# Transposes moved ahead of the scale columns, and a norm ahead of their read, in the first phase of a fused attention and MLP kernel

## Chip, cores, metric

One core of one Trainium2 chip. The time is device time in microseconds (us) of one execution. "Granted clock" is the share of its full clock that the profile says TensorE was given; "landing" is the time at which the last completion record of a transfer came in. TensorE (PE) does matmuls and transposes, VectorE (DVE), ScalarE (ACT) and GpSimd (POOL) do elementwise work, SyncE (SP) issues transfers.

## The reference

A transformer block with modulation (2048 rows of 1024, 32 query heads, 4 key/value heads, bf16):

```python
mod = (_silu(c) @ w_mod).reshape(c.shape[0], 6, 1, -1)
sa, ca, ga, sb, cb, gb = (mod[:, i] for i in range(6))      # shortened
h = _layernorm(x) * (1 + ca) + sa
x = x + ga * A(h)            # q = h @ wq, windowed attention, @ wo
h = _layernorm(x) * (1 + cb) + sb
x = x + gb * B(h)            # silu(h @ w_gate) * (h @ w_up) @ w_down
```

What matters is the start: the layernorm of the first 512 rows (four row tiles of 128), its transpose, the scale columns 1 + ca, and the first q projection.

## The kernel before

The first transfers go to one queue in this order. The first load holds row tiles 0 and 1, the second tiles 2 and 3, and `load_wm(1, 0)` is a megabyte of w_mod for the first half of ca:

```python
for i in range(QT // 2):
    load_x2(i)
for half in range(DH):
    load_wm(1, half)
    load_wq8(2 * half)
    load_wq8(2 * half + 1)
load_wm(0, 0)
...
load_wm(0, 1)
```

The stretch that is changed. `norm_*(t, half)` norms half of tile t, `xpose_0(t, n, half)` is four PE transposes (L962), `mod_cols` is 32 one-column matmuls (L786) and a VectorE read of their result (L789), `warm` issues dummy matmuls, `h_scale` (L1045) makes the operand of q:

```python
norm_pool(1, m1[:, 4:5], slice(0, 512))
...
norm_dve(2, 0)
warm(2)
rstd_0(mv[3])
norm_act(1, m1[:, 5:6], 1)
xn_tile(3)
norm_dve(3, 0)
mod_cols(1, 0, ca1, True)          # waits for the first megabyte of w_mod
...
norm_dve(2, 1)
norm_act(3, m3[:, 4:5], 1)
xpose_0(1, xn0[1], 0)
xpose_0(2, xn0[2], 0)
xpose_0(3, xn0[3], 0)
xpose_0(1, xn0[1], 1)
...
h_scale(0, h0_ps[0][:, 0, :])      # needs the columns and all first-half transposes
...
for dt in range(4):
    for g in range(4, H0):
        q0(g, (dt,))               # the q projection, L1065
```

The instructions keep this order on each engine.

Of the kernel before, what the change touches and what calls it, by code (L numbers as in the profile page):

```python
# [588 lines left out]
def fast_path(ctx, tc, flag, A_x, A_k_cache, A_v_cache, A_wq, A_wo, B_x, B_w_gate, B_w_up,  # L589
# [59 lines left out]
    def mm(name, shape=(P, 512), dt=FP32):  # L649
        return psp.tile(list(shape), dt, name=name, tag="mm", bufs=4)  # L650
# [107 lines left out]
    def warm(n):  # L758
        for _ in range(n):
            nc.tensor.matmul(warm_ps, lhsT=ones_bf, rhs=warm_w, start=True, stop=True)  # L760
# [20 lines left out]
    def mod_cols(vec, half, dst, add_one, tiles=(0, 1, 2, 3)):  # L781
        wm = wm_tiles[(vec, half)]
        ps = mm("mod_ps", (P, 4))
        for i in tiles:
            for dt in range(DT):
                nc.tensor.matmul(ps[:, i:i + 1], lhsT=wm[:, dt, i * P:(i + 1) * P],  # L786
                                 rhs=siluc[:, dt:dt + 1], start=(dt == 0), stop=(dt == DT - 1))
        i0, i1 = tiles[0], tiles[-1] + 1
        nc.vector.tensor_scalar(out=dst[:, 4 * half + i0:4 * half + i1], in0=ps[:, i0:i1],  # L789
                                scalar1=1.0 if add_one else 0.0, scalar2=None, op0=ALU.add)  # L790
# [168 lines left out]
    def xpose_0(t, n, half):  # L959
        for i in range(4):  # L960
            dt = 4 * half + i
            nc.tensor.transpose(h0_ps[half][:, i, t * P:(t + 1) * P],  # L962
                                n[:, dt * P:(dt + 1) * P], ident)
# [5 lines left out]
    xn0 = {}  # L969

    def rstd_0(m):
        nc.scalar.activation(out=m[..., 2:3], in_=m[..., 1:2], func=ACT.Ln, bias=eps_t)
        nc.scalar.activation(out=m[..., 2:3], in_=m[..., 2:3], func=ACT.Exp, scale=-0.5)

    def xn_tile(t):
        xn0[t] = wk.tile([P, D], BF16, name="xn", tag="xn", bufs=3)

    def norm_dve(t, half):
        sl = slice(half * 512, half * 512 + 512)
        nc.vector.tensor_scalar(out=xn0[t][:, sl], in0=xt[t][:, sl], scalar1=mv[t][:, 0:1],  # L980
                                scalar2=mv[t][:, 2:3], op0=ALU.subtract, op1=ALU.mult)
# [5 lines left out]
    def norm_act(t, minus, half):  # L987
        sl = slice(half * 512, half * 512 + 512)
        nc.scalar.activation(out=xn0[t][:, sl], in_=xt[t][:, sl], func=ACT.Identity, bias=minus,
                             scale=mv[t][:, 2:3])  # L990
# [23 lines left out]
    for t in (1, 2):  # L1014
# [3 lines left out]
                            op0=ALU.mult, op1=ALU.mult)  # L1018
    norm_dve(2, 0)
    warm(2)  # L1020
    rstd_0(mv[3])
    norm_act(1, m1[:, 5:6], 1)
    xn_tile(3)
    norm_dve(3, 0)
    mod_cols(1, 0, ca1, True)
    nc.gpsimd.tensor_scalar(out=m3[:, 4:5], in0=mv[3][:, 0:1], scalar1=-1.0, scalar2=mv[3][:, 2:3],
                            op0=ALU.mult, op1=ALU.mult)
    norm_dve(2, 1)
    norm_act(3, m3[:, 4:5], 1)
    xpose_0(1, xn0[1], 0)  # L1030
    xpose_0(2, xn0[2], 0)
    xpose_0(3, xn0[3], 0)
    xpose_0(1, xn0[1], 1)
    xpose_0(2, xn0[2], 1)
# [432 lines left out]
def kernel(tc, *args):  # L1467
    nc = tc.nc
    with tc.tile_pool(name="guard", bufs=1) as gp:
        flag = gp.tile([1, 1], I32, name="flag")  # L1470
        over = fast_path(tc, flag, *args)
        with tc.If(over > 0):
            general_path(tc, *args)
# [30 lines left out]
```

## Time and profile before

| | before |
|---|---|
| median of the first three runs | 1271.33 us (1271.32 to 1271.65) |
| the run whose profile is shown | 1271.83 us, span 1270.0 us |
| PE busy, granted clock | 1262.1 us, 0.999 |
| all PE waits | 3.3 us, all before 9.7 us |

### The profile page before, as it was taken

The page shows a single profiled execution, that of the slowest core. Times are in us where ns is not written, and L with a number is a line of the kernel's source. Part 1 is how long each engine was busy: PE and PEld are TensorE (multiplying, and loading weights), DVE is VectorE, ACT ScalarE, POOL GpSimd, SP SyncE. Part 2 cuts the span into 40 slices and gives each one's busy share as a digit, 9 for nine tenths or more (in the row PEclk, how much of TensorE's full clock was granted, in tenths as well). Part 3 has the DMA queues.
Part 4 walks back from the last instruction along what each step waited for, and adds up shares of the span by engine and source line. Part 5 has one row for each costly group of instructions (what it writes and reads, how often), then busy time and mean ns, then how long its engine had stood idle before and what let it go on. Part 6 is the DMA issues. An engine that isn't in the chain of part 4 may idle for free.

```text
span 1270.0 us, 18153 instructions
## 1 busy us (share of the span) xinstructions
PE 1262.1 (99%) x7587; PEld 641.2 (50%) x7587; DVE 609.0 (48%) x1331; ACT 336.3 (26%) x440; POOL 4.3 (0%) x17
## 2 busy tenths in 40 slices
PE   8999999999999999999999999999999999999998
PEld 4555555555555555555554444444444444444444
DVE  5665658785678664677564631311222112221122
ACT  4543334343333433334341111011100111011100
POOL 1000000000000000000000000000000000000000
PEclk9999999999999999999999999999999999999999
DMA  9897657678556655455585479336633565425702
GB/s 292 206 259 171 168 141 176 168 162 211 128 136 175 150 137 153 113 154 113 120 206 143 137 225 248 95 95 208 215 114 105 169 213 182 158 91 169 246 16 70
DMA packets 306763, 204.45 MB, mean 161 GB/s; under 512 B 145521, under 2 KB 303217, under 8 KB 306674
## 3 DMA queue, kind: packets, MB, share of 16 engines
q1 hardware_dynamic: 301762, 199.03, 58.2%
q10 hardware_dynamic: 4912, 4.20, 1.0%
q8 instruction: 61, 1.00, 0.3%
q14 instruction: 28, 0.23, 0.1%
HBM read 165.94 MB, written 4.21 MB: 134 GB/s over the span
## 4 chain that ended last, share of the span: by engine, by line
PE 99%; DMA 1%; SPq 0%; DVE 0%; issue 0%
PE gu_ps L1380 30%; PE a_ps L1298 17%; PE q_ps L1223 16%; PE d_ps L1400 15%; PE o_ps L1266 9%; PE s_ps L1234 9%; PE q_ps L1065 1%; DMA wm<-in_w_mod_dram 1%; PE mod_ps L786 0%; PE one_ps L1083 0%; PE h_ps L962 0%; PE one_ps L1076 0%; SPq L664 0%; PE q_ps L1129 0%; DVE f L1404 0%
## 5 line engine op out<-in xcount | busy, mean ns | idle before, releaser
L1236 ACT ACTIVATE pT<-s_ps 128x1024 bf16<-128x1024 f32 x256 | 249.4, 1020 | 347.5 <-PE s_ps L1234 347.5
L1298 PE MATMUL a_ps<-wo,oT 128*128 128x512 bf16 x1024 | 241.9, 379 | 0.0
L1223 PE MATMUL q_ps<-hT,wq 128*128 128x512 bf16 x960 | 227.1, 379 | 0.0
L1386 DVE TENSOR_TENSOR guT<-gu_ps,sg 128x512 bf16<-128x512 f32 x112 | 77.5, 692 | 287.8 <-ACT sg L1385 287.8
L1380 PE MATMUL gu_ps<-hT,wg 128*128 128x512 bf16 x896 | 211.7, 379 | 0.0
L1385 ACT ACTIVATE sg<-gu_ps 128x512 bf16<-128x512 f32 x112 | 66.9, 597 | 488.7 <-PE gu_ps L1380 482.9
L1400 PE MATMUL d_ps<-wd,guT 128*128 128x512 bf16 (+2 forms) x952 | 194.2, 366 | 0.0
L1380 PE MATMUL gu_ps<-hT,wu 128*128 128x512 bf16 x672 | 163.3, 379 | 0.0
L1298 PEld LDWEIGHTS <-oT 128*128 128x128 bf16 x1024 | 100.2, 98 | 120.6
L947 DVE CAST qT<-q_ps 128x512 bf16<-128x512 f32 x121 | 83.6, 691 | 154.7 <-PE q_ps L1223 154.4
L1223 PEld LDWEIGHTS <-wq 128*128 128x128 bf16 x960 | 93.9, 98 | 113.3
L1400 PEld LDWEIGHTS <-guT 128*128 128x128 bf16 x952 | 90.9, 98 | 102.9
L1266 PEld LDWEIGHTS <-pT 128*128 128x128 bf16 x2048 | 126.6, 98 | 30.2
L1380 PEld LDWEIGHTS <-wg 128*128 128x128 bf16 x896 | 87.7, 98 | 105.5
L1266 PE MATMUL o_ps<-v_sb,pT 128*128 128x129 bf16 x2048 | 137.0, 220 | 0.0
L1234 PE MATMUL s_ps<-qT,kT 128*128 128x512 bf16 x512 | 131.5, 379 | 0.0
L1380 PEld LDWEIGHTS <-wu 128*128 128x128 bf16 x672 | 65.7, 98 | 79.3
L1253 DVE TENSOR_TENSOR oq<-o_ps,rl 128x256 bf16<-128x256 f32 (+2 forms) x256 | 100.6, 419 | 3.9
L1404 DVE TENSOR_TENSOR f<-d_ps,gb_bc 128x512 f32<-128x512 f32 (+2 forms) x34 | 22.4, 660 | 140.8 <-PE d_ps L1400 140.8
L1234 PEld LDWEIGHTS <-kT 128*128 128x128 bf16 x512 | 44.9, 98 | 30.9 <-issue 0.5
L1306 DVE TENSOR_TENSOR acc<-a_ps,acc 128x512 f32<-128x512 f32 x64 | 44.0, 688 | 32.6 <-PE a_ps L1298 32.6
L1380 PE MATMUL gu_ps<-hT,v_sb 128*128 128x512 bf16 x224 | 57.5, 379 | 0.0
(106 smaller groups left out, 427.0 us busy)
## 6 DMA issues: line engine op xcount, KB each, us to landing
wq<-in_A_wq_dram SPq DMA_DIRECT2D x64, 512.0 KB
wo<-in_A_wo_dram SPq DMA_DIRECT2D x64, 512.0 KB
wg<-in_B_w_gate_dram SPq DMA_DIRECT2D x56, 512.0 KB
wd<-in_B_w_down_dram SPq DMA_DIRECT2D x56, 512.0 KB
wu<-in_B_w_up_dram SPq DMA_DIRECT2D x42, 512.0 KB
v_sb<-in_B_w_up_dram SPq DMA_DIRECT2D x14, 512.0 KB
x<-in_A_x_dram SPq DMA_DIRECT2D x8, 512.0 KB
wm<-in_w_mod_dram SPq DMA_DIRECT2D x4, 1024.0 KB
```

What stands on the lines that cost most here:

```text
L947: nc.vector.tensor_copy(out=t, in_=q_ps)
L1223: nc.tensor.matmul(q_ps, lhsT=w, rhs=hT[("h1", cc)][:, dt, :], start=(dt == 0), stop=(dt == DT - 1))
L1234: nc.tensor.matmul(s_ps[:, i, :], lhsT=kT[:, kv, j * P:(j + 1) * P], rhs=qT[g], start=True, stop=True)
L1236: nc.scalar.activation(out=p[:, 2 * jj:2 * jj + 2, :], in_=s_ps, func=ACT.Exp, scale=scale)
L1253: nc.vector.tensor_tensor(out=dst, in0=ps[:, s0:s0 + cnt, 0:Dh], in1=sc, op=ALU.mult)
L1266: nc.tensor.matmul(o_slot["ps"][:, s_, :], lhsT=pT[g][:, j, t * P:(t + 1) * P], rhs=v_sb[:, kv, j, 0:VN], start=(j == 0), stop=(j == WT - 1))
L1298: nc.tensor.matmul(a_ps, lhsT=oT[(cc, 2 * q + i)][:, hh % 4, t * P:(t + 1) * P], rhs=wo_tiles[(cc, q, dh, i)][:, hh % 4, :], start=(hh == ...
L1306: nc.vector.tensor_tensor(out=acc[(cc, t)][:, dsl], in0=a_ps, in1=acc[(cc, t)][:, dsl], op=ALU.add)
L1380: nc.tensor.matmul(ps[:, n, :], lhsT=gu_w[(cc, fg, nm, dt // 4)][:, dt % 4, fi * P:(fi + 1) * P], rhs=hT[("h2", cc)][:, dt, :], start=(dt ...
L1385: nc.scalar.activation(out=g, in_=ps[:, 0, :], func=ACT.Silu)
L1386: nc.vector.tensor_tensor(out=guT[(cc, fg)][:, fi, :], in0=ps[:, 1, :], in1=g, op=ALU.mult)
L1400: nc.tensor.matmul(d_ps, lhsT=guT[(cc, f // 4)][:, f % 4, t * P:(t + 1) * P], rhs=wd_tiles[(cc, dh, f // 4)][:, f % 4, c0:c0 + w], start=( ...
```

## The change

The intent is to do ready transposes while PE waits for the w_mod block, and to keep VectorE from holding up the scaling.

```diff
     norm_dve(2, 0)
     warm(2)
+    xpose_0(1, xn0[1], 0)
+    xpose_0(2, xn0[2], 0)
     rstd_0(mv[3])
     norm_act(1, m1[:, 5:6], 1)
     xn_tile(3)
     norm_dve(3, 0)
+    norm_dve(2, 1)
     mod_cols(1, 0, ca1, True)
     nc.gpsimd.tensor_scalar(out=m3[:, 4:5], ...)   # cut
-    norm_dve(2, 1)
     norm_act(3, m3[:, 4:5], 1)
-    xpose_0(1, xn0[1], 0)
-    xpose_0(2, xn0[2], 0)
     xpose_0(3, xn0[3], 0)
```

## The prediction

> **What bounds the kernel now.** I read the busy shares first, then who waited for whom, then the chain that ended last, then the timeline of the stretch that the diff touches. The page's first part says which engine sets the end:
>
> ```profile
> PE 1262.1 (99%) x7587; PEld 641.2 (50%) x7587; DVE 609.0 (48%) x1331; ACT 336.3 (26%) x440; POOL 4.3 (0%) x17
> ```
>
> TensorE (PE) is busy for 1262.1 of 1270.0 us. About 3.3 us of the rest are three waits, which are all that the list of waits, filtered to PE, has for the whole span (columns: engine, line and tile, releaser, us in total, times, longest):
>
> ```profile
> PE warm_ps L760 <- DVE warm_w L749: 1.6, 1, 1.6
> PE h_ps L962 <- POOL xn L984: 1.1, 1, 1.1
> PE mod_ps L786 <- DMA wm<-in_w_mod_dram: 0.6, 1, 0.6
> ```
>
> All three lie in the first 10 us. After 9.68 us PE waits for nothing until its last matmul. So an instruction there can be worth something in one way only: PE must reach the point from which it runs unbroken sooner, and nothing later may take that back. The chain that ended last, in its stretch from 9 us on (start, duration, what), shows how this point is reached:
>
> ```profile
> 1.74 7.90 DMA wm<-in_w_mod_dram
> 9.64 0.04 issue
> 9.68 0.95 PE mod_ps L786 x32
> 10.63 1.36 PE h_ps L962 x24
> 12.00 4.38 PE q_ps L1065 x20
> ```
>
> The first megabyte of w_mod lands at 9.64 us. Then follow the 32 tiny matmuls that make half of the scale columns (L786), then 24 transposes of the normed rows (L962), then the q projection (L1065). This is the stretch in question. Its timeline (start, duration, engine, line, operation, output<-input, shapes, count, idle before):
>
> ```profile
> 8.38 0.77 POOL L984 TENSOR_SCALAR xn<-x,mv 128x512 bf16<-128x512 bf16 x1 [0.43 <-ACT mv L973]
> ...
> 8.72 0.58 DVE L980 TENSOR_SCALAR xn<-x,mv 128x512 bf16<-128x512 bf16 x1
> ...
> 9.46 0.42 DVE L980 TENSOR_SCALAR xn<-x,mv 128x512 bf16<-128x512 bf16 x1 [0.16 <-POOL mv L1017]
> 9.46 1.52 ACT L989 ACTIVATE xn<-x,mv 128x512 bf16<-128x512 bf16 x2
> ...
> 9.68 0.95 PE L786 MATMUL mod_ps<-siluc,wm 128*128 128x1 bf16 x32 [0.62 <-DMA wm<-in_w_mod_dram]
> ...
> 10.50 1.50 PE L962 MATMUL h_ps<-ident,xn 128*128 128x128 bf16 x24
> 10.67 0.16 DVE L789 TENSOR_SCALAR modT<-mod_ps 128x4 f32<-128x4 f32 x1 [0.80 <-PE mod_ps L786]
> 10.75 0.40 DVE L980 TENSOR_SCALAR xn<-x,mv 128x512 bf16<-128x512 bf16 x1
> 11.37 1.27 DVE L1045 TENSOR_SCALAR hs<-h_ps,modT 128x512 bf16<-128x512 bf16 x3 [0.21 <-PE h_ps L962]
> ...
> 11.90 0.59 PE L1065 MATMUL q_ps<-hs,wq 128*128 128x512 bf16 x2
> ```
>
> The first-half norm of row tile 1 (POOL) is done at 8.38 + 0.77 = 9.15 us and that of tile 2 (VectorE) at 8.72 + 0.58 = 9.30 us. Their transposes could run from there, but stand in PE's order behind the L786 group, which waits for its weights until 9.68 us. PE is idle for 0.62 us beside ready work.
>
> **What the Trainium skill says.** "TensorE: Matmul & The Clock Gate", Part 2, "Step-by-step: what each phase is for", has weight loads pulled ahead of running matmuls, but the matmuls themselves in program order. The trace agrees: the ready transposes stayed behind the waiting L786. The same page, Part 1, "Wait — 56ns, not 53.3ns?", gives about 56 ns from start to start of warm 128-column matmuls and a floor of about 25 ns for very small ones. The trace agrees roughly: (11.90 - 10.50) / 24 = 58 ns for the transposes, (10.50 - 9.68) / 32 = 26 ns for L786. Part 4, "PE-mode transpose", has about 275 ns for a transpose within a kernel and says that the fast clock does not engage for it; here the 32 transposes have a median of 219 ns at a granted clock of 1.00, so I take the trace. The same page, "Engine queue depths", calls VectorE strictly first in, first out; that agrees with the tile 2 norm at 10.75 us, right behind the read of L789, though VectorE had nothing to do from 9.88 to 10.67 us.
>
> **The change part by part.** No instruction is added or removed. The listing of instruction order shows eight transposes (with their eight weight loads) moved ahead of the L786 group on PE, one norm moved ahead of the L789 read on VectorE, and ACT, POOL and the DMA queue in the same order.
>
> 1. Eight transposes go into the gap. POOL released PE earlier in the trace within 0.05 us (7.95 to 8.00), so they start at about 9.15 + 0.05 = 9.20 us. At 57 ns each, the last starts at 9.20 + 7 x 0.057 = 9.60 us, and PE is free for the next at about 9.66 us. The first of tile 2 is due at 9.43 us, after its data (9.30). L786 thus starts at 9.68 us as before, when its weights are there: the eight are hidden. Cost 0 to 0.03 us.
> 2. After L786, 16 transposes remain instead of 24: PE could begin q at 10.50 + 16 x 0.058 = 11.43 us instead of 11.90 us, 0.47 us sooner.
> 3. VectorE must follow, since q reads what L1045 writes. Before, L1045 began at 11.37 us, when the twelfth transpose was done (10.50 + 11 x 0.057 + 0.22 = 11.35). Now only the four first-half transposes of tile 3 follow L786: 10.50 + 3 x 0.057 + 0.22 = 10.89 us. The other condition is the read of the columns, 10.67 + 0.16 = 10.83 us; where the same read is followed by its user with nothing between (17.19 + 0.16 = 17.35, user at 17.46), 0.11 us pass, so 10.94 us. This one ends last. L1045 starts at 10.94 instead of 11.37 us: 0.43 us sooner.
> 4. That needs VectorE free, hence the moved norm. It takes 0.40 us at 9.88 to 10.28 us, in idle time, instead of 10.75 to 11.15 us. Left where it was, it would hold L1045 until about 11.15 us and half the gain would be lost.
> 5. One L1045 takes 0.48 us and PE started 0.05 us after its end (11.37 + 0.48 = 11.85, q at 11.90). New start of q: 10.94 + 0.48 + 0.05 = 11.47 us. The smaller of 0.47 and 0.43 counts: PE starts its unbroken run 0.43 us sooner. Sum: 1271.33 - 0.43 = 1270.90 us.
>
> **The rivals.**
> (a) A later transfer takes the place of the wait. The w_mod and wq loads go on at 340 to 385 GB/s and don't come sooner because PE is sooner. The trace's completion records (I read these times directly; no printed view lists them) have the next blocks landing at 10.99 and 12.38 (wq), 15.38 (w_mod), 21.68 and 24.78 us (w_mod), and PE's first weight loads from them at 11.78, 12.98, 16.00, 22.41 and 25.40 us: slack 0.79, 0.60, 0.62, 0.74 and 0.62 us. All exceed 0.43, by 0.17 us at the least. For it: a transfer that lands 0.3 us later in some run would give back 0.1 us. Against it: PE has no such wait now. If true, 1271.0 to 1271.2 us.
> (b) The eight transposes start late and push L786 past 9.68 us. POOL's spans are rough. If PE saw tile 1 only at 9.40 us, L786 would move by 0.2 us, the column read with it, and 0.2 us would be left: 1271.1 us. If the POOL wait were longer than the DMA wait, it would be the new first wait and the time could rise; with 9.15 against 9.68 us I see no sign of it.
> (c) The start is bought but given back later, where VectorE, ACT or the DMA queue pace PE. PE is 99% busy and has no wait after 9.68 us, which speaks against it. Loads that reuse a buffer are issued when PE releases it, so they move along; those that don't are the ones in (a). If true, 1271.3 us, no change.
> (d) The gain is larger, as a full 0.62 us of idle time is filled. Against it: only eight transposes, 8 x 0.057 = 0.46 us, are put there. At most 1270.85 us.
>
> **Range and chances.** The point is step 5. The three runs before span 0.33 us (1271.32 to 1271.65) and the median sits at the low end, so the reading itself can be off by 0.15 us either way. Rivals (a) and (b) move it up by 0.1 to 0.3 us; (d) down by 0.05 us. I take 1270.60 to 1271.35 us, which holds a complete loss of the gain at its upper end. 2% is 25 us; nothing in this change is in reach of it in either direction, and I leave half a per cent on each side for what I have not seen.
>
> **What would show it right or wrong.** In the profile after: eight L962 at about 9.20 us, their wait named POOL; L786 still at 9.68 to 9.71 us, idle before it under 0.1 us in place of 0.62; three L980 on VectorE before L789; L1045 at 10.94 us; the first q matmul at 11.47 us; every later piece of the chain 0.43 us sooner, and no new PE wait. Step 1 is wrong if L786 starts after 9.75 us; step 3 if L1045 starts near 11.1 us or later; rival (a) is right if PE waits for wm or wq after 12 us; rival (c) if q starts at 11.5 us but the last matmul does not end 0.4 us sooner.

## The result, and the profile after

| six runs each, same rounds | median | lowest to highest |
|---|---|---|
| before | 1271.42 us | 1271.27 to 1273.02 |
| after | 1271.66 us | 1271.43 to 1272.19 |

The ratio is 1.000 with a 95% interval of 0.9987 to 1.0013. Ratios and intervals are worked out from the runs of the same rounds; they are not the ratio of the medians. The prediction of 1270.90 us was wrong: 1271.66 lies above its range, and no gain is to be seen.

Yet the profile after looks as predicted. Its timeline over the same stretch:

```profile
8.31 0.77 POOL L984 TENSOR_SCALAR xn<-x,mv 128x512 bf16<-128x512 bf16 x1 [0.43 <-ACT mv L973]
...
9.14 0.62 PE L962 MATMUL h_ps<-ident,xn 128*128 128x128 bf16 x8 [0.15 <-POOL xn L984]
9.39 0.74 DVE L980 TENSOR_SCALAR xn<-x,mv 128x512 bf16<-128x512 bf16 x2 [0.16 <-POOL mv L1017]
...
9.60 0.94 PE L786 MATMUL mod_ps<-siluc,wm 128*128 128x1 bf16 x32
...
10.40 1.05 PE L962 MATMUL h_ps<-ident,xn 128*128 128x128 bf16 x16
10.58 0.16 DVE L789 TENSOR_SCALAR modT<-mod_ps 128x4 f32<-128x4 f32 x1 [0.45 <-PE mod_ps L786]
10.85 1.66 DVE L1045 TENSOR_SCALAR hs<-h_ps,modT 128x512 bf16<-128x512 bf16 x4
...
11.38 1.89 PE L1065 MATMUL q_ps<-hs,wq 128*128 128x512 bf16 x8
```

Eight transposes run first, L786 follows without a wait, 16 transposes remain, and q starts at 11.38 us instead of 11.90. The list of waits on PE has lost its DMA entry:

```profile
PE warm_ps L760 <- DVE warm_w L749: 1.6, 1, 1.6
PE h_ps L962 <- POOL xn L984: 1.0, 2, 0.9
```

The chain that ended last no longer begins at a transfer in this stretch. It goes through POOL's norm, and further back to the first load of x, which landed at 4.40 us:

```profile
8.31 0.78 POOL xn L984
9.10 0.05 issue
9.14 0.62 PE h_ps L962 x8
9.76 0.78 PE mod_ps L786 x32
```

And the 0.52 us (11.90 - 11.38) arrive at the end. The last matmul group in the chain, first in the kernel before, then in the kernel after:

```profile
1216.94 48.50 PE d_ps L1400 x280
```

```profile
1216.42 48.50 PE d_ps L1400 x280
```

So this pair of profiles differs by 0.52 us and the medians differ by 0.24 us the other way. The completion records of the transfers in the two traces hold the key. A load counts as landed when the last of its 16 completions is in. In the profile before, 15 of the 16 for the w_mod block came between 8.36 and 8.75 us and the last at 9.64 us. In the profile after, all 16 were in at 8.76 us. PE was released 0.04 us after the sixteenth, which agrees with the Trainium skill, "DMA: Bandwidth & Descriptors", "Why a DMA increments its semaphore by 16 and not by 1": only the full 16 mean that all data has landed. I had compared an execution with a late block with one in which it was early.

### The profile page after: what moved, and what is told of

Its sections match the earlier page's. It is cut to its first block, busy times and chain, and to the rows that moved or that the text cites. A ratio compares the mean times of both kernels' runs of the same rounds, so it can differ in the third digit from the quotient of the medians. Undisturbed runs are those within 1.5% of the kernel's fastest.

```text
span 1269.5 us, 18153 instructions
## 1 busy us (share of the span) xinstructions
PE 1262.3 (99%) x7587; PEld 641.2 (51%) x7587; DVE 608.6 (48%) x1331; ACT 336.3 (26%) x440; POOL 4.3 (0%) x17
## 4 chain that ended last, share of the span: by engine, by line
PE 99%; DMA 0%; DVE 0%; ACT 0%; POOL 0%; issue 0%
PE gu_ps L1380 30%; PE a_ps L1298 17%; PE q_ps L1223 16%; PE d_ps L1400 15%; PE o_ps L1266 9%; PE s_ps L1234 9%; PE q_ps L1065 1%; DMA x<-in_A_x_dram 0%; PE mod_ps L786 0%; PE one_ps L1083 0%; PE h_ps L962 0%; PE one_ps L1076 0%; DVE st L846 0%; ACT junk L1005 0%; POOL xn L984 0%; ACT mv L972 0%
```

## The experiments

Theory: the gain is only as large as the wait for the block, that wait differs from execution to execution, and where there is none the new order costs something. Rival 1: the gain is real in every execution and given back later. Rival 2: noise alone. Each group of runs (e1 to e4, e5 to e8, e9 to e12) had its own chip; each experiment is set against runs of its own chip.

### e1 and e2: both kernels again, unchanged

> The kernel before, unchanged, for a second profile of it. Theory (the gain hangs on when the first w_mod block lands; the profile on which I predicted caught a late landing, 9.64 us, in a run 0.50 us slower than the median of its kernel): in most executions the block lands near 8.8 us as in the profile of the changed kernel; then L786 starts by 9.1 us, q at about 11.3 to 11.4 us and the span is about 1269.4 to 1269.6 us. Rival 1 (the gain is real in every execution but given back later): q starts at about 11.9 us again, span about 1270. Rival 2 (noise alone): the time differs by up to 0.7 us from run to run with the first 12 us the same.

> The changed kernel again. Theory: q at 11.35 to 11.5 us whether the block lands early or late, span 1269.4 to 1269.7 us, median within 0.25 us of the kernel before. If a later block (w_mod at 21.6 or 24.7 us) lands some tenths later, a new PE wait there. Rival 1: q at 11.4 us and the end not 0.4 us sooner than in a run of the kernel before whose q starts at 11.9. Rival 2: no pattern.

Five runs each: e1 has a median of 1271.89 us (1271.23 to 1273.82), e2 1272.05 us (1271.56 to 1274.61); nine runs of the kernel before beside them 1271.87 us. The ratios to these are 1.0003 (0.9989 to 1.0016) and 1.0008 (0.9995 to 1.0022).

The profile of e1 missed every expectation. It is a run of 1273.82 us; its PE timeline:

```profile
9.96 0.96 PE L786 MATMUL mod_ps<-siluc,wm 128*128 128x1 bf16 x32 [0.78 <-DMA wm<-in_w_mod_dram]
10.78 2.72 PE L962 MATMUL h_ps<-ident,xn 128*128 128x128 bf16 x24
13.29 4.02 PE L1065 MATMUL q_ps<-hs,wq 128*128 128x512 bf16 x16
```

The block landed at 9.91 us, not near 8.8. And the 24 transposes took 2.72 us where they took 1.50. The view of stretches (us and busy time of each engine, then the granted clock, DMA share and GB/s) says why:

```profile
9.00:10.68 1.68, 0.91 (x30) 0.73 (x30) 0.84 (x2) 1.56 (x4) 0.82 (x3) 1.00 1.02 376
10.68:14.10 3.42, 3.42 (x36) 2.92 (x33) 2.32 (x7) 0.99 (x2) 0.00 (x0) 0.50 1.08 359
```

For 3.41 us (10.68 to 14.10) the granted clock was 0.50. That is a second source of spread which I had not thought of. In e2, x landed at 4.62 us (4.40 in the profile after) and q started at 11.62 us, 0.12 us outside what I expected.

### e3 and e4: the block loaded later

```diff
-    for half in range(DH):
-        load_wm(1, half)
-        load_wq8(2 * half)
-        load_wq8(2 * half + 1)
+    load_wq8(0)
+    load_wm(1, 0)
+    load_wq8(1)
+    ...                         # the rest in the same order as before
```

> The kernel before, with the first w_mod block loaded behind the first wq block instead of ahead of it, so that it lands about 1.5 us later in every execution (10.1 to 11.0 us). Theory: L786 at 10.2 to 11.0, q about 2.2 us after that (12.4 to 13.2), time 1.0 to 1.8 us over the kernel before: 1272.4 to 1273.2.

> The changed kernel with the same later load. Theory: now the wait that the change hides work in is there in every execution, so it gains about 0.45 us on e3 (8 transposes of 57 ns): q about 1.8 us after L786, and the median 0.3 to 0.6 us under e3. Rival 1 (given back later): q 0.45 us sooner after L786, but the time within 0.15 us of e3. Rival 2: no difference clear of noise.

Both missed: e3 has a median of 1276.61 us (1273.10 to 1277.15), e4 1275.20 us (1274.55 to 1277.01). In the profile of e4 PE waited 1.88 us for the block, and the clock was at 0.50 from 13.30 to 16.71 us; in that of e3 it reached full speed only at 10.95 us. The clock differs between the profiles, so the times of this pair decide nothing about the change. The distances from the landing of the block to q do agree with what follows: 2.27 us in e3 (11.41 to 13.68) and 1.89 us in e4 (11.72 to 13.61, the last 0.31 us at half clock). e7 and e8 repeat it with PE kept busy.

### e5 and e6: no wait for the block

```diff
-                nc.tensor.matmul(ps[:, i:i + 1], lhsT=wm[:, dt, i * P:(i + 1) * P],
+                nc.tensor.matmul(ps[:, i:i + 1],
+                                 lhsT=zeros if (vec, half) == (1, 0) else wm[:, dt, i * P:(i + 1) * P],
```

The scale columns are wrong on purpose here. All transfers stay.

> The kernel before with the first scale columns made from a resident tile of zeros instead of the loaded w_mod block (the result is wrong on purpose; all transfers stay, no wait on one is left at that place). This is the earliest possible landing. Theory, as revised (the gain is the size of the landing wait, and where there is none the changed order must wait for the POOL norm before the columns): L786 at 8.9 to 9.1 us with no idle named DMA, q at 11.2 to 11.4 us, i.e. at least as early as in the changed kernel's profile (11.38). Time within 0.3 us of the kernel before. Rival (given back later): q start still 0.4 us later than in e6.

> The changed kernel with the same resident zeros (wrong result on purpose). Theory: L786 stands behind the eight transposes and these behind the POOL norm, so L786 at 9.55 to 9.65 us, q at 11.4 to 11.5 us: 0.1 to 0.2 us later than in e5, and the time 0 to 0.2 us longer. Rival (the gain is there in every execution): 0.4 us sooner than e5.

PE timelines, e5 first, then e6:

```profile
8.93 0.94 PE L786 MATMUL mod_ps<-siluc,zeros 128*128 128x1 bf16 x32
9.73 1.74 PE L962 MATMUL h_ps<-ident,xn 128*128 128x128 bf16 x24
11.31 0.59 PE L1065 MATMUL q_ps<-hs,wq 128*128 128x512 bf16 x2
```

```profile
9.37 0.62 PE L962 MATMUL h_ps<-ident,xn 128*128 128x128 bf16 x8 [0.15 <-POOL xn L984]
9.83 0.94 PE L786 MATMUL mod_ps<-siluc,zeros 128*128 128x1 bf16 x32
...
11.61 0.59 PE L1065 MATMUL q_ps<-hs,wq 128*128 128x512 bf16 x2
```

With nothing to wait for, the old order is the better one. It runs L786 in the time in which POOL is still norming tile 1, and q starts at 11.31 us. What q then follows is ScalarE's second norm (L989), on which the last four transposes wait; e5's chain:

```profile
10.22 0.81 ACT xn L989
...
11.07 0.40 PE h_ps L962 x4
```

The new order must first wait for POOL and starts q at 11.61 us. Of these 0.30 us, 0.12 are a later landing of x (4.62 against 4.50 us); 0.18 us are the order's own, as far as one profile of each can tell. The medians are 1271.39 us (1271.29 to 1271.59) and 1271.63 us (1271.48 to 1272.53): 0.24 us apart, the wrong way for the change, though the intervals (0.9982 to 1.0009 and 0.9986 to 1.0013) overlap. e5's median is 0.34 us under the kernel before beside it, where I had expected at most 0.3; e6's q start was 0.11 us later than I had expected, its difference in sign and about in size as expected.

### e7 and e8: a late block, PE kept busy

As e3 and e4, with eight more dummy matmuls (in e7 `warm(10)` for `warm(2)`, in e8 `warm(8)` behind the eight transposes).

> The kernel before with the first w_mod block loaded behind the first wq block, as in e3, and eight more dummy matmuls (0.216 us each) ahead of the columns, so that TensorE is not idle for long and its clock is not taken down. Theory: e3 and e4 were ruled by the half clock; here the clock stays full from about 7 us on, PE waits 0.3 to 1.0 us for the block at 11.2 to 11.7 us, q about 2.25 us after L786, at 13.4 to 14 us. Time 1273 to 1273.8, with a spread under 1 us.

> The changed kernel with the same late block and the same eight dummies behind the eight transposes. Theory: the transposes lie in time that PE waits for anyway, so q comes about 1.8 us after L786, and the median is 0.3 to 0.5 us under e7. Rival (given back later): within 0.15 us of e7 although q is sooner after L786. Rival (noise): no difference.

PE timelines, e7 first, then e8. Their lines are numbered one or two higher:

```profile
11.41 0.95 PE L788 MATMUL mod_ps<-siluc,wm 128*128 128x1 bf16 x32 [0.69 <-DMA wm<-in_w_mod_dram]
...
13.62 0.59 PE L1067 MATMUL q_ps<-hs,wq 128*128 128x512 bf16 x2
```

```profile
11.80 0.95 PE L788 MATMUL mod_ps<-siluc,wm 128*128 128x1 bf16 x32
...
13.59 0.59 PE L1068 MATMUL q_ps<-hs,wq 128*128 128x512 bf16 x2
```

From the landing of the block (11.36 and 11.75 us) to q it is 2.26 us in e7 and 1.84 us in e8: the gain of 0.42 us, as predicted for a block that is waited for. The times follow: 1274.00 us (1273.67 to 1274.70) against 1273.59 us (1273.36 to 1273.77), 0.41 us between medians of five runs each on one chip, and four of the five runs of e8 are below all of e7's. The intervals (1.0003 to 1.0030 and 0.9998 to 1.0026) are too wide to tell the two apart, so the weight lies on the distances in the traces. e7's median is 0.2 us above the range I had expected. The clock stayed full in both profiles from about 7 us on. The filling is what differs from e3 and e4: PE's idle time before the block was 1.06 and 1.88 us there, 0.69 and 0.14 us here, and the mean clock of the ten runs was 0.997 to 0.999 there, 0.999 to 1.000 here. Rival 1 falls: where there is a wait, the gain reaches the end.

### e9 and e10: one part alone

As e8 with the norm of tile 2 left behind the columns; as e7 with that norm moved and the transposes left.

> As e8 (late block, eight dummies), with the transposes moved but the tile 2 norm left behind the read of the columns. By step 4 of the prediction the scaling L1045 is held until that norm is done, about 0.2 us: q about 2.0 us after L786 and the time 0.15 to 0.25 us over e8 (1273.6), so 1273.8. Rival (the norm does not matter): as e8.

> As e7 (late block, eight dummies), with the norm moved but the transposes left behind the columns. Theory: L1045 waits for the twelfth transpose either way, so nothing is gained: q about 2.2 us after L786, time as e7 (1274.0) within 0.15 us. Rival (the norm alone brings a part): 0.2 us under e7.

In e9, q started at 14.07 us, 2.03 us after the block (12.04 us): 0.19 us of the 0.42 are lost without the norm. The chain has the norm ahead of the last transposes, so it holds PE itself, and not only the scaling that step 4 named (two lines of the chain, then q in the timeline):

```profile
13.23 0.33 DVE xn L982
...
13.61 0.62 PE h_ps L964 x8
```

```profile
14.07 1.46 PE L1068 MATMUL q_ps<-hs,wq 128*128 128x512 bf16 x6
```

In e10 q started at 13.86 us, 2.26 us after the block (11.60 us), just as in e7: the norm alone brings nothing.

```profile
13.86 1.67 PE L1067 MATMUL q_ps<-hs,wq 128*128 128x512 bf16 x7
```

The median of e10 is 1274.11 us, as expected. That of e9 is 1274.19 us, 0.4 us over what I expected; its profile shows a block 0.29 us later than e8's. The medians of e9 and e10 do not show the 0.23 us by which e9 should be ahead: in the profiles e9's block landed 0.44 us later than e10's, and five runs each may not average such differences out. Both ran on another chip than e7 and e8. So the verdict rests on the distances within the traces, one profile each.

### e11 and e12: a third profile of each kernel

> The kernel before, a third profile of it, for when the first w_mod block lands. Theory: q at the later of 11.3 us (landing up to about 9.05) and landing + 2.26, as long as the clock is full; the span ends 1258.1 us after q starts. Rival (given back later): the distance from the start of q to the end is not constant.

> The changed kernel, a third profile. Theory: q at the later of about 2.24 us after POOL's half norm ends (11.4 to 11.6 us, the norm with the landing of x) and landing + 1.87; the span ends 1258.1 us after q starts. Rival (given back later): that distance is longer than in the kernel before.

e11 (1271.72 us): the block landed at 9.38 us and q started at 11.65 us, 2.27 us later, as expected. e12 (1271.85 us), the changed kernel, on PE:

```profile
9.70 0.62 PE L962 MATMUL h_ps<-ident,xn 128*128 128x128 bf16 x8 [0.15 <-POOL xn L984]
...
10.15 0.94 PE L786 MATMUL mod_ps<-siluc,wm 128*128 128x1 bf16 x32
...
11.94 0.59 PE L1065 MATMUL q_ps<-hs,wq 128*128 128x512 bf16 x2
```

The w_mod block was there at 9.34 us and was not waited for. The first load of x had landed at 4.95 us, 0.55 us later than in the profile after. Everything behind it, POOL's norm included, was late by as much. That is 0.34 us past the 11.4 to 11.6 us that I had expected, and 2.29 us after the end of POOL's norm (9.65), as in the profile after (9.09 to 11.38). The new order had swapped one landing for another.

### The full-clock profiles of the two orders

x and w_mod are landings, all in us; "rest" is the time less the start of q.

| profile | x | w_mod | q starts | q - x | q - w_mod | time | rest |
|---|---|---|---|---|---|---|---|
| before | 4.46 | 9.64 | 11.90 | 7.44 | 2.26 | 1271.83 | 1259.93 |
| e11 before | 4.36 | 9.38 | 11.65 | 7.29 | 2.27 | 1271.72 | 1260.07 |
| e5 before, no wait | 4.50 | not used | 11.31 | 6.81 | | 1271.29 | 1259.98 |
| e7 before, late | 4.40 | 11.36 | 13.62 | | 2.26 | 1273.68 | 1260.06 |
| after | 4.40 | 8.76 | 11.38 | 6.98 | 2.62 | 1271.43 | 1260.05 |
| e2 after | 4.62 | 9.70 | 11.62 | 7.00 | 1.92 | 1271.56 | 1259.94 |
| e12 after | 4.95 | 9.34 | 11.94 | 6.99 | 2.60 | 1271.85 | 1259.91 |
| e6 after, no wait | 4.62 | not used | 11.61 | 6.99 | | 1271.57 | 1259.96 |
| e8 after, late | 4.57 | 11.75 | 13.59 | | 1.84 | 1273.59 | 1260.00 |

The rest is 1259.9 to 1260.1 us in each of them: nothing is given back after q has started. Each order fits a simple rule:

- before: q starts at the later of x + 6.81 and w_mod + 2.26;
- after: q starts at the later of x + 6.99 and w_mod + 1.84.

Three of the four terms have two profiles or more behind them (2.26 or 2.27 in four with e3; 1.84 in e8, near it in e4; 6.98 to 7.00 in four). The 6.81 comes from e5 alone, and with it the 0.18 us below.

The change takes 0.42 us off the path from w_mod and adds 0.18 us to that from x. It gains up to 0.42 us where the block comes more than about 4.73 us after x (6.99 - 2.26), and loses up to 0.18 us where it comes sooner. Landings were seen in eight profiles with the original load order (the block 9.64, 8.76, 9.91, 9.70, 9.30, 8.96, 9.38 and 9.34 us; x 4.46, 4.40, 4.59, 4.62, 4.50, 4.62, 4.36 and 4.95 us, in the order before, after, e1, e2, e5, e6, e11, e12). The rules give gains of 0.42, -0.18, 0.42, 0.35, 0.07, -0.18, 0.29 and -0.18 us for them, on average 0.13 us. That is an estimate for full clock, from few profiles. It is 0.01% of the time, and the intervals of the timed runs are over ten times wider.

The timed runs do not contradict this, and cannot confirm it. The lowest of 39 runs of the kernel before is 1271.23 us and the lowest of 12 of the changed kernel 1271.43 us, 0.20 us apart: close to the 0.18 us that the new order costs where the block is early, but the numbers of runs and the chips differ. Five of the 39 and one of the 12 are over 1273 us. Four of these six (e1's two among them) have a mean clock of 0.998, and no other run of the two kernels whose clock is on record is below 0.999; one of the six has 0.999, and for one no clock is on record. So the half clock likely explains four of them; a profile shows it only in e1.

One thing the rules leave open. Between 1272.15 and 1273 us lie four of 17 runs of the new order (1272.19 in the result, 1272.79 in e2, 1272.53 and 1272.24 in e6) and one of 44 of the old (e5 counted in). None of them was profiled. A later landing of x would do it, and so would a clock that rises late: in e3 it rose at 10.95 us and the mean clock is 0.999 all the same. Which it was is not shown, nor whether the new order brings it about.

Whether another order of these instructions beats both was not tried.

## Why the prediction was wrong

- **Step 1 failed** ("L786 thus starts at 9.68 us as before, when its weights are there: the eight are hidden"). It took the landing of one execution for a property of the kernel. The last of 16 completions came at 8.76 to 9.91 us in eight profiles. By the rules above the eight transposes are hidden in some of these executions, partly hidden in some, and in three of the eight the new order costs 0.18 us. In the profile after, L786 started at 9.60 us, 0.84 us after its block had landed: it waited for the moved transposes, and these for POOL.
- **The sum in step 5 failed with it** ("1271.33 - 0.43"). The 0.43 us come from a profile of a run of 1271.83 us and were taken off the median of 1271.33 us. The faster runs had no such long wait to begin with. For the profiled run itself the step was sound: with its landings the rules give a start of q at 11.48 us instead of 11.90, and 1271.83 - 0.42 = 1271.41 us.
- **Steps 2, 3 and 4 were right** for an execution that waits: 0.42 us in e7 and e8 against 0.43, and without the norm 0.19 us of it are lost in e9, where step 4 said half. Step 4 had the hold on the scaling alone; in e9 it is also on the last transposes.
- **Rival (a)** had the right kind of cause, a transfer, and the wrong ones: no profile of the changed kernel with the original loads has a PE wait on a later w_mod or wq block. It was the load of x, ahead of the block, that took its place, in all four of these profiles (after, e2, e6, e12).
- **Rival (b)** came close: it asked what happens if POOL's release is later than the block, and dismissed it on the strength of 9.15 against 9.68 us from one trace. In e12 it was 9.65 against 9.34 us.
- **Rival (c)** is refuted by the constant rest, and (d) is not seen where the landings are allowed for: of the 0.52 us between the two profiles the rules give 0.42 to the order, and the rest to an x that was 0.06 us earlier and a block that was early. (Its sum has a slip: 1271.33 - 0.46 is 1270.87, not 1270.85.)
- **The range** rested on a spread of 0.33 us in three runs. Over 51 runs of the two kernels it is 3.4 us (1271.23 to 1274.61). The landings, seen 1.15 us (w_mod) and 0.59 us (x) apart, and the clock make up a part of that; how much each is not shown.
- **The chances** (99% within 2%) were right.

So the failed step is shown in traces; that it is also why the medians of the timed runs show no gain is an inference from eight profiles. What stays open: how often each landing occurs, so the sign of the mean effect; the runs of 1272.2 to 1272.8 us; and whether the new order, with less idle time on PE, makes the half clock rarer.

## What to carry to other kernels

Before you take a gain off a median, look where the profiled run lies among the timed ones: a wait that ends on a transfer may be a feature of that one execution. Work out for both orders what each start depends on (here two landings) and let each of them vary; a reorder that moves work ahead of one wait can put another wait in front of it. When the expected gain is some tenths of a microsecond, force the wait to be long in one pair and absent in another, and compare distances within the traces.

## What the Trainium skill lacked or had wrong

- "DMA: Bandwidth & Descriptors" describes the 16 completions, and its section on latency calls two of the engines usually slower, but no figure says how far apart the completions may come. For the same 1 MB load in eight profiles, the first of the 16 came at 8.25 to 8.40 us and the last at 8.76 to 9.91 us.
- "TensorE: Matmul & The Clock Gate", "Why this matters for your kernels", asks for no idle gap over some 3 us to keep the clock. In e1 the clock fell to 0.50 at 10.68 us, and the list of waits has no gap over 0.78 us from 2 us on. It fell for 3.41 us, which agrees with the window of 3413 ns that the page's Part 1 gives. What activity counts there no run here shows.
- The same page, Part 4, has a transpose within a kernel at about 275 ns without the fast clock. Whether L962 carries the transpose mode that the page speaks of, the trace does not say; it lists them as MATMUL. Here the median was 219 ns, started every 58 ns at a granted clock of 1.00, and under the half clock in e1 24 of them took 2.72 us instead of 1.50, so here the clock does rule them.
